# Attention values as one whole-array matmul a head plus 64x64 quarters, in one operation with the next tile's scores

## The chip, the cores and the metric

The kernel runs on one core of a Trainium2 chip. A core has a matrix engine (TensorE, PE in the profile; its weight loads are PEld), VectorE (DVE), ScalarE (ACT), GpSimd (POOL) and SyncE (SP), each with its own instruction stream, and 16 DMA engines that all queues share. The metric is the device time of one execution in microseconds (us), as the median of the runs. The profile is one further execution, taken by the hardware profiler; its span goes from the first to the last instruction.

## What is computed

Attention with a causal window of 128 keys and four sink keys (the first four of the sequence, which every query sees), over 4 batches, 8 heads, 768 positions, head size 64. Its output, with the heads side by side as 512 columns, goes through a layer norm, a two-layer MLP with 2048 hidden units and relu, and a residual.

```python
scores = scale * np.matmul(q, k.transpose(0, 1, 3, 2))
keep = is_sink | in_window                 # pos_k < 4, or 0 <= pos_q - pos_k < 128
a = softmax(np.where(keep, scores, -1e9))
attn_out = np.matmul(a, v)
...
xn = (x - mu) / np.sqrt(var + 1e-06) * g_ln
ch = np.maximum(xn @ w_ch1, 0.0) @ w_ch2
return x + ch
```

## The kernel before

A *tile* is 128 positions of one batch: 24 tiles (NT), six a batch (RB), numbered t; r is the tile's place in its batch. Two tiles are a *chunk* c, 12 in all (NC), three a batch (RC); R is the chunk's place in its batch, so R=0 opens one.

**Attention of a chunk** (chunks 2 to 11, `attend`; the four tiles of chunks 0 and 1 have `attend_tile`). Scores are computed transposed, with keys on the partitions and queries on the columns. For two of the four head pairs at a time (`half`), `bands` issues matmuls of 64 keys by 64 head dimensions (line 663): the two heads of a pair use the two row halves of the array, the two halves of the keys its two column halves, so that four run in the quarters of the array. Only blocks that touch the window are computed. With R=0, line 750 does it with 128 keys on 64 rows instead. The first half also computes the sinks' scores (line 754). The exponentials go to the tiles `pe` (line 764), a mask clears what lies outside the window (line 768), and `value` multiplies by V: for each head two whole-array matmuls of 65 columns (line 798), one over the own 128 keys and one over the 128 before, the 65th column of V being ones, which gives the row sum; and before them one 260-column matmul per four heads for the sinks (line 793, `vs` holding the sink values). In the first tile of a batch there is only one block of keys.

**After the values.** VectorE takes reciprocals (line 811), scales (813), takes the statistics (817, 819) and centres (821); POOL computes the inverse deviation (826, 827). The centred x is transposed, by TensorE in chunks 0 to 2 (834) and by a DMA on SP's queue from chunk 3 (836, by way of line 542), to `xnt`. q and k are transposed by TensorE up to chunk 3 (639) and by DMAs on SP's queue from chunk 4 (626).

**MLP of a chunk** (`mlp`): eight groups of eight matmuls for the first layer (line 867; 860 in chunk 0), each followed by a relu on ACT or DVE (877, 879); then for each tile four groups of four matmuls of 512 columns for the second layer (896), which DVE combines with the residual (904) and SP's queue stores (908).

**Loads.** q, k, v and the weights are loaded on POOL's queue, which casts to bf16 (lines 521, 524, 548, 600, 625, 634). The gain vector g is loaded transposed as 512 single elements (505).

**What sets the order.** Nothing is scheduled by hand: `Plan` holds every operation with its engine, an estimated duration, a priority and the buffers that it uses, and `Plan.run` walks through time, picks for each engine the ready operation of best priority within a short window, and hands out buffer slots. The operations are then emitted in order of their planned start, and each engine runs its own in that order, waiting on semaphores where data or a buffer isn't ready. `nb` is an earliest planned start. From priority `strict` on, TensorE's operations keep the order of their priorities. Priorities are in steps of 16 a chunk: `at(c, step)` is 16c - 8 plus an entry of `PAR`, and the MLP of a chunk starts at 16c + 8.5.

**PSUM.** Eight banks: two pairs of banks (`pair`, for scores and, from chunk 2, the values) and four single ones (`one`, for the MLP's layers, transposes and the sinks' scores).

Of the kernel before, what the change touches and what calls it, by code (L numbers as in the profile page):

```python
# [7 lines left out]
FP32 = mybir.dt.float32  # L8
# [5 lines left out]
class Buf:  # L14


    def __init__(self, name, ring=None):
        self.name, self.ring = name, ring
        self.writers, self.users = [], []
        self.slot = None  # L20
        self.left = 0

# [42 lines left out]
class Plan:  # L65
# [7 lines left out]
    SHARED = 36.0  # L73
# [8 lines left out]
    def op(self, name, engs, prio, emit, reads=(), writes=(), rw=(), dma=None, after=(), mode="n", hold=(), nb=0.0):  # L82
# [10 lines left out]
        o.bufs = list(dict.fromkeys(list(reads) + list(writes) + list(rw) + list(hold)))  # L93
# [19 lines left out]
    def run(self):  # L113
# [8 lines left out]
        while ready:  # L122
# [5 lines left out]
            for o in ready:  # L128
# [4 lines left out]
                for b in need:  # L133
# [9 lines left out]
                    avail = max(avail, s.free_at)  # L143
# [68 lines left out]
def fix(occ, extra=0.09):  # L212
# [3 lines left out]
SW = (0.9, 0.7, 0.9)  # L216
SW_W = (2.65, 0.7, 0.9)
# [4 lines left out]
HW_T = (0.10, 0.8, 0.8)  # L222
# [6 lines left out]
PAR = dict(strict=40.0, win=0.4, tr=-8.0, sc=-5.0, sc1=-2.0, av=2.0, trx=9.0, by_dma=4, x_by_dma=3,  # L229
           w1p=(1.6, 2.6, 2.7, 2.8), pm=3, w2p=(4.5, 4.51, 4.52, 4.53), apart=2, vs0=(2.0, 13.0), by_tile=1, vp=(0.0, 0.1, 2.0, 2.1, 4.55, 4.56), ld1=0.05)  # L230
# [135 lines left out]
def kernel(  # L366
# [63 lines left out]
    mask, mask0 = const("mask", [128, 2, 4, 128], BF16), const("mask0", [128, 2, 3, 128], BF16)  # L430
# [3 lines left out]
    vs = [const(f"vs{b}", [128, H, 65], BF16) for b in range(B)]  # L434
    gt = const("gt", [128, NDM], FP32)
# [9 lines left out]
    names = ("ident_f", "ident", "upper", "neg", "mask", "mask0", "sel", "vc", "vcd", "gt", "junk", "tab", "mhalf", "ones_f")  # L445
# [37 lines left out]
    def masks0(e):  # L483
        up = upper.unsqueeze(1).to_broadcast([128, 2, 128])
        V.tensor_copy(mask0[:, :, 0, :], up)
        V.tensor_scalar(mask0[:, :, 1, :], up, -1.0, 1.0, op0=ALU.mult, op1=ALU.add)
        V.tensor_copy(mask0[:, :, 2, :], up)
        V.memset(mask0[0:NS, :, 0:2, :], 1.0)

    def negs(e):  # L490
# [4 lines left out]
    constant("masks0", "DVE", 0.9, 6.1, masks0, ["upper"], writes=[Bc["mask0"]], nb=27.5)  # L495
# [4 lines left out]
        op=ALU.add, axis=mybir.AxisListType.X), ["ident"], writes=[Bc["sel"]])  # L500
    constant("mhalf", "DVE", 0.06, -52, lambda e: V.memset(mhalf, -0.5), writes=[Bc["mhalf"]])
# [3 lines left out]
    P.op("gt", {"SP": (0.4, 0.4)}, 3.0, lambda e: nc.sync.dma_start(gt, moe_g_ln.rearrange("(j p) -> p j", p=128)),  # L505
         writes=[Bc["gt"]], dma=HW_T)
# [5 lines left out]
    for b in range(B):  # L512
        P.op(f"vs{b}", {"DVE": dve(520)} if b else {"POOL": (0.9, 1.0)}, PAR["vs0"][0] if b == 0 else 48.0 * b - 20, lambda e, b=b: (V if b else G).tensor_tensor(
            vs[b], vc[:, b, :].unsqueeze(1).to_broadcast([128, H, 65]),
            sel.unsqueeze(2).to_broadcast([128, H, 65]), op=ALU.mult),
            reads=[Bc["vcd"], Bc["vc"], Bc["sel"]], writes=[Bvs[b]], nb=PAR["vs0"][1] if b == 0 else 40.0 * b)

    w1prio = PAR["w1p"]
# [25 lines left out]
    def load_v(t, prio):  # L544
# [5 lines left out]
            writes=[bv], dma=SW, after=list(ones_of.values()))  # L550
# [6 lines left out]
    def chunk(c):  # L557
# [57 lines left out]
        else:  # L615
            for nm, src, bT in (("k", k, kT_b), ("q", q, qT_b)):
# [3 lines left out]
                for i in range(2):  # L620
                    if c >= PAR["by_dma"]:
# [3 lines left out]
                             lambda e, nat=nat, ap=ap: G.dma_start(nat.t, ap), writes=[nat], dma=SW)  # L625
# [27 lines left out]
        for i in range(2):  # L653
            load_v(2 * c + i, ld + 0.3 + 0.1 * i if c >= RC else PAR["vp"][2 * c + i])
# [351 lines left out]
```

## Time and profile before

| | us |
|---|---|
| median of 3 runs | 220.07 (219.91 to 220.21) |
| profiled execution | 220.3 |
| its span | 218.7 |
| TensorE matmuls busy | 211.0 |
| VectorE busy | 117.9 |
| ScalarE busy | 108.2 |
| GpSimd busy | 90.2 |

The busy share of a stretch and the clock that TensorE was granted, in 40 slices of the span, in tenths:

```profile
PE   6889999999999999999999999999999999999993
DVE  5489845595797725725715815725716715732011
ACT  3768465145447447445546447445546447441610
POOL 7998673798091813463550722570110110120000
PEclk9999999999999999999999999999999999999998
DMA  5999999999999999799897999997523421121103
```

The granted clock is near full throughout (mean 0.997). The DMA engines are busy nine tenths or more of most slices up to some 155 us. The busiest groups of instructions:

```profile
L896 PE MATMUL one<-w,h 128*128 128x512 bf16 (+1 forms) x400 | 89.0, 371 | 0.0
L867 PE MATMUL one<-xnt,w 128*128 128x256 bf16 x704 | 82.4, 273 | 0.0
L798 PE MATMUL pair<-vn,pe 128*128 128x65 bf16 x296 | 12.2, 193 | 0.0
L663 PE MATMUL pair<-qT,kT 64*64 64x64 bf16 (+2 forms) x400 | 8.9, 219 | 0.1
L548 POOL DMA_DIRECT2D vn<-in_v_dram x24 | 21.9, 921 | 3.3 <-DMA w<-in_moe_w_ch_dram 3.1
```

A group's line gives the source line, the engine, what is written from what, and how often; then the busy time in us, the mean duration of one in ns, and the engine's idle time before them. Matmuls are pipelined: one of 512 columns lasts 0.37 us from start to end, while the next starts 0.216 us after it.

### The profile page before, as it was taken

The numbers are of one execution on the slowest core, as the hardware profiler recorded it, in microseconds if no ns is written. First come the engines' busy times: TensorE is split into PE (matmuls) and PEld (weight loads), VectorE is DVE, ScalarE is ACT, GpSimd is POOL, SyncE is SP. The second block draws the span as 40 slices with busy tenths as digits, with TensorE's granted clock in tenths as the row PEclk, the third lists the DMA queues.
The fourth block names the chain that finished last, engine by engine and source line by source line (L and its number), as shares of the span: only waits on it lengthen the run. The fifth ranks groups of instructions, "written<-read, shape, count | busy, mean of one in ns | idle before, by whom it ended". The sixth has DMA issues, their size and how long they took to land.

```text
span 218.7 us, 5474 instructions
## 1 busy us (share of the span) xinstructions
PE 211.0 (97%) x2233; PEld 144.6 (66%) x2233; DVE 117.9 (54%) x269; ACT 108.2 (49%) x162; POOL 90.2 (41%) x131
## 2 busy tenths in 40 slices
PE   6889999999999999999999999999999999999993
PEld 2557875764965964964965964964965965965852
DVE  5489845595797725725715815725716715732011
ACT  3768465145447447445546447445546447441610
POOL 7998673798091813463550722570110110120000
PEclk9999999999999999999999999999999999999998
DMA  5999999999999999799897999997523421121103
GB/s 155 163 183 207 176 206 197 156 211 154 179 159 163 139 120 129 100 160 145 139 135 116 133 115 129 135 140 106 129 40 98 107 41 48 51 48 51 48 12 101
DMA packets 108576, 27.47 MB, mean 126 GB/s; under 512 B 99200, under 2 KB 105600, under 8 KB 108544
## 3 DMA queue, kind: packets, MB, share of 16 engines
q0 software_dynamic: 74944, 13.11, 83.7%
q1 hardware_dynamic: 32544, 13.41, 30.2%
q10 hardware_dynamic: 1056, 0.52, 0.9%
q8 instruction: 19, 0.31, 0.6%
q14 instruction: 13, 0.11, 0.2%
HBM read 27.30 MB, written 6.29 MB: 154 GB/s over the span
## 4 chain that ended last, share of the span: by engine, by line
PE 90%; DVE 6%; issue 1%; ACT 1%; DVEq 0%
PE one L896 39%; PE one L867 35%; PE pair L798 4%; PE pair L663 3%; PE pair L962 2%; PE pair L793 1%; DVE st L817 1%; PE pair L750 1%; DVE x L813 1%; DVE xc L821 1%; DVE xnt L845 1%; PE one L639 1%; PE one L860 1%; PE one L834 1%; PE one L754 1%
## 5 line engine op out<-in xcount | busy, mean ns | idle before, releaser
L896 PE MATMUL one<-w,h 128*128 128x512 bf16 (+1 forms) x400 | 89.0, 371 | 0.0
L877 ACT ACTIVATE h<-one 128x512 bf16<-128x512 f32 x95 | 56.6, 598 | 59.1 <-PE one L867 50.7
L867 PE MATMUL one<-xnt,w 128*128 128x256 bf16 x704 | 82.4, 273 | 0.0
L867 PEld LDWEIGHTS <-w 128*128 128x128 bf16 x704 | 67.4, 98 | 10.2
L896 PEld LDWEIGHTS <-h 128*128 128x128 bf16 x400 | 37.3, 98 | 38.2 <-issue 0.9
L768 DVE TENSOR_TENSOR pe<-pe,mask 128x1024 bf16<-128x1024 bf16 (+1 forms) x40 | 26.0, 649 | 54.7 <-ACT pe L764 53.8
L764 ACT ACTIVATE pe<-pair 128x1024 bf16<-128x1024 f32 (+1 forms) x40 | 36.2, 957 | 33.4 <-PE pair L663 21.6
L625 POOL DMA_DIRECT2D nat<-in_k_dram x16 | 14.2, 890 | 36.8 <-DMA kT<-nat 28.1
L904 DVE SCALAR_TENSOR_TENSOR ot<-one,st,x 128x512 f32<-128x512 f32 (+1 forms) x25 | 18.1, 725 | 15.2 <-PE one L896 15.1
L826 POOL TENSOR_SCALAR st<-st 128x1 f32<-128x1 f32 x24 | 7.1, 297 | 43.4 <-DVE st L819 42.2
L548 POOL DMA_DIRECT2D vn<-in_v_dram x24 | 21.9, 921 | 3.3 <-DMA w<-in_moe_w_ch_dram 3.1
L625 POOL DMA_DIRECT2D nat<-in_q_dram x16 | 14.6, 913 | 12.9 <-DMA qT<-nat 12.0
L817 DVE BATCH_NORM_STATS2 st<-x 128x6 f32<-128x512 bf16 x24 | 16.7, 695 | 0.8
L798 PEld LDWEIGHTS <-pe 128*128 128x128 bf16 x352 | 14.0, 97 | 2.1 <-ACT pe L709 0.6
L827 POOL TENSOR_TENSOR st<-st,mhalf 128x1 f32<-128x1 f32 x24 | 14.3, 596 | 2.0
L813 DVE TENSOR_TENSOR x<-pair,rec 128x512 bf16<-128x512 f32 x20 | 13.8, 691 | 0.7
L798 PE MATMUL pair<-vn,pe 128*128 128x65 bf16 x296 | 12.2, 193 | 0.0
L663 PEld LDWEIGHTS <-kT 64*64 64x64 bf16 x400 | 6.2, 107 | 6.3 <-issue 6.1
L821 DVE TENSOR_SCALAR xc<-x,st 128x512 bf16<-128x512 bf16 x24 | 9.3, 389 | 0.9
L811 DVE RECIPROCAL rec<-pair 128x8 f32<-128x8 f32 x20 | 4.0, 202 | 9.7 <-PE pair L798 9.7
L709 ACT ACTIVATE pe<-pair 128x1024 bf16<-128x1024 f32 (+1 forms) x8 | 7.3, 919 | 3.5 <-PE pair L663 2.1
L663 PE MATMUL pair<-qT,kT 64*64 64x64 bf16 (+2 forms) x400 | 8.9, 219 | 0.1
(87 smaller groups left out, 127.4 us busy)
## 6 DMA issues: line engine op xcount, KB each, us to landing
out_dram<-ot SPq DMA_DIRECT2D x23, 256.0 KB
w<-in_moe_w_ch_dram POOLq DMA_DIRECT2D x8, 512.0 KB, 12.9
vn<-in_v_dram POOLq DMA_DIRECT2D x24, 128.0 KB, 6.3
nat<-in_k_dram POOLq DMA_DIRECT2D x22, 128.0 KB, 6.1
nat<-in_q_dram POOLq DMA_DIRECT2D x22, 128.0 KB, 6.2
natf<-in_k_dram SPq DMA_DIRECT2D x2, 256.0 KB
natf<-in_q_dram ACTq DMA_DIRECT2D x2, 256.0 KB
xnt<-xc SPq DMA_TRANSPOSE x18
```

The source lines that it names most:

```text
L548: P.op(f"vld{t}", {"POOL": (0.87, 0.9)}, prio, lambda e: G.dma_start(bv.t[:, :, 0:64], v[b, :, 128 * r:128 * (r + 1), :].rearrange("h p d ...
L625: lambda e, nat=nat, ap=ap: G.dma_start(nat.t, ap), writes=[nat], dma=SW)
L663: nc.tensor.matmul(pp.t[64 * kh:64 * kh + 64, h2, col + off:col + off + n], lhsT=kt.t[rs, hp, k0 + 64 * kh:k0 + 64 * kh + 64], rhs=qT.t[rs ...
L764: P.op(f"ex{c}{hp}", {"ACT": act(2 * n)}, d + 0.1 + 0.05 * j, lambda e, pp=pp, pb=pb: nc.scalar.activation(pb.t[:, :, 0:n], pp.t[:, :, 0:n ...
L768: V.tensor_tensor(pb.t[:, :, 0:n], pb.t[:, :, 0:n], mm, op=ALU.min if R else ALU.mult),
L798: nc.tensor.matmul(bank(h // 4)[:, 65 * (h % 4):65 * (h % 4) + 65], lhsT=part(h, n), rhs=vn_b[tv].t[:, h, :], start=(not R and h % 4 == 0 ...
L813: P.op(f"x{t}{run[0]}", {"DVE": dve(512 * share)}, dd + 0.11, lambda e, pv=pv, rc=rc, run=run: V.tensor_tensor(x.t[:, 256 * run[0]:256 * r ...
L817: P.op(f"bn{t}", {"DVE": fix(0.60)}, d + 0.12, lambda e: V.bn_stats(st.t[:, 8:14], x.t), reads=[x], writes=[st, mv])
L867: nc.tensor.matmul(ph.t[:, 256 * s:256 * s + 256], lhsT=w1[ht // 4][:, j, 128 * (ht % 4):128 * (ht % 4 + 1)], rhs=xnt.t[:, j, :], start=j ...
L877: nc.scalar.activation(hb.t, ph.t, AF.Relu)
L896: nc.tensor.matmul(pc.t[:, 0:wd], lhsT=(h1[2 * s + i].t[:, 128 * ii:128 * ii + 128] if by_tile else h1[ht // 2].t[:, 256 * (ht % 2) + 128 ...
L904: V.scalar_tensor_tensor(ot.t[:, sl], in0=pc.t[:, 0:wd], scalar=st.t[:, 16:17], in1=x.t[:, sl], op0=ALU.mult, op1=ALU.add),
```

## The change

For chunks 3 to 11 (batches 2 to 4) `attend` is replaced by `block`, one operation a tile. `block(t)` first finishes the values of tile t-1 and then computes the scores of tile t; `block(NT)` closes with values alone. `attend` stays for chunk 2.

The keys of a tile are regrouped. With 64-key halves, the queries' own tile has the halves 0 and 1 and the tile before it -2 and -1. Halves -1 and 0 are seen, in part, by all 128 queries: they are the *middle 128 keys*, stacked on the 128 partitions, and one whole-array matmul a head covers them. Half -2 matters only to the first 64 queries and half 1 only to the last 64: each is a 64x64 quarter. For heads 0 to 3 (u=0) and 4 to 7 (u=1) the two halves are stacked in opposite order, so that the quarters of both use all four quarters of the array. The sinks' values become four quarters of 260 columns, for which the sink values are also kept with their halves swapped (`vs_s`, made by six DMAs on SP's queue). V is loaded in the shifted stacking by `load_m`, in three or four DMAs a tile.

The exponentials and masks of a tile cover 768 columns in two instructions each; the masks are a product with `band` or, in a batch's first two tiles, `edge`, built by `bands3`. The first tile of a batch also runs the middle matmul and half of the quarters over keys of the batch before, with zeros in the masked places. The sinks' scores of a chunk are computed with its first tile.

PSUM now has three pairs; the third is two of the four single banks, which the planner lends (`lent`) to operations that come before the next waiting `block`. Second-layer sums from chunk 2 on use only the two others (`acc`). `lag` lets a score bank be handed out although it comes free a little after the operation's start. `strict` is raised, so that the order of priorities no longer binds TensorE; loads of V from tile 10 and of q and k from chunk 5 are planned no earlier than 58 us; the transposes of chunk 4 no longer wait for the scores of chunk 3. The gain vector is loaded as four rows and transposed by TensorE.

```diff
-        o.bufs = list(dict.fromkeys(list(reads) + list(writes) + list(rw) + list(hold)))
+        o.bufs = sorted(dict.fromkeys(list(reads) + list(writes) + list(rw) + list(hold)), key=lambda b: b.ring != "pair")
...
-                    avail = max(avail, s.free_at)
+                    avail = max(avail, s.free_at - b.lag)
...
+PAR = dict(strict=400.0, late=58.0, win=0.4, tr=-8.0, sc=-5.0, sc1=-2.0, av=2.0, blk=-8.0, step=6.0, trx=9.0, by_dma=4, x_by_dma=3,
...
-    pairs = [psum.tile([128, 2, 512], FP32, name=f"pair{i}") for i in range(2)]
-    ones = [psum.tile([128, 512], FP32, name=f"one{i}") for i in range(4)]
-    P.ring("pair", [Slot(pairs[i], f"pair{i}", banks[2 * i:2 * i + 2]) for i in range(2)])
-    P.ring("one", [Slot(ones[i], f"one{i}", [banks[4 + i]]) for i in range(4)])
+    pairs = [psum.tile([128, 2, 512], FP32, name=f"pair{i}") for i in range(3)]
+    ones = [pairs[2][:, i, :] for i in range(2)] + [psum.tile([128, 512], FP32, name=f"one{i}") for i in range(2, 4)]
+    P.ring("two", [Slot(pairs[i], f"two{i}", banks[2 * i:2 * i + 2]) for i in range(2)])
+    P.ring("pair", [Slot(pairs[i], f"pair{i}", banks[2 * i:2 * i + 2]) for i in range(3)])
+    P.ring("one", [Slot(ones[i], f"one{i}", [banks[4 + i]], rank=0, lent=i < 2) for i in range(4)])
+    P.ring("acc", [Slot(ones[i], f"acc{i}", [banks[4 + i]]) for i in range(2, 4)])
...
+    def bands3(e):
+        for u in range(2):
+            m = edge[1][u]
+            for g in range(2):
+                rows = slice(64 * g, 64 * g + 64)
+                up, at = upper[rows, 64 * g:64 * g + 64], [0, 128] if g == u else [128, 64]
+                V.tensor_copy(m[rows, at[0]:at[0] + 64], up)
+                V.tensor_scalar(m[rows, at[1]:at[1] + 64], up, -1.0, 1.0, op0=ALU.mult, op1=ALU.add)
+                V.memset(m[rows, 64:128] if g == u else m[rows, 0:64], 1.0)
+            own = 64 * u
+            V.tensor_copy(band[u], m.unsqueeze(1).to_broadcast([128, 4, 192]))
+            V.tensor_copy(edge[0][u], m)
+            V.memset(m[own:own + NS, 128:192], 0.0)
+            V.memset(edge[0][u][64 - own:128 - own, 0:128], 0.0)
+            V.memset(edge[0][u][own:own + 64, 128:192], 0.0)
+            V.memset(edge[0][u][own:own + NS, 0:128], 1.0)
...
+    constant("bands3", "DVE", 3.0, 6.1, bands3, ["upper"], writes=[Bc["band"]], nb=28.0)
...
+    P.op("gt", {"SP": (0.4, 0.4)}, 3.0, lambda e: nc.sync.dma_start(g_rows, moe_g_ln.rearrange("(j p) -> j p", p=128)),
+         writes=[gr_b], dma=HW_T)
+    P.op("gtt", pe(0.1), PAR["gtt"], lambda e: nc.tensor.transpose(gt_p.t[:, 0:NDM], g_rows, ident_f[0:NDM, 0:NDM]),
+         reads=[gr_b, Bc["ident_f"]], writes=[gt_p])
+    P.op("gtc", {"DVE": fix(0.07)}, PAR["gtt"] + 0.1, lambda e: V.tensor_copy(gt, gt_p.t[:, 0:NDM]), reads=[gt_p], writes=[Bc["gt"]])
...
+    Bvt = [None] + [Buf(f"vt{b}") for b in range(1, B)]
+    for b in range(1, B):
+        for g in range(2):
+            P.op(f"vt{b}{g}", {"SP": (0.35, 0.4)}, 48.0 * b - 19.5, lambda e, b=b, g=g: nc.sync.dma_start(
+                vs_s[b][64 * g:64 * g + 64], vs[b][64 * (1 - g):64 * (1 - g) + 64]), reads=[Bvs[b]], writes=[Bvt[b]], dma=HW_V)
...
-            writes=[bv], dma=SW, after=list(ones_of.values()))
...
+    def load_m(t, prio):
...
+        if r:
+            parts = [(0, 128, hi, at(b, s0 - 64, 128, hi)), (0, 64, lo, at(b, s0, 64, lo)), (64, 64, lo, at(b, s0 - 64, 64, lo))]
+        else:
+            pb = (t - 1) // RB
+            parts = [(0, 64, hi, at(pb, S - 64, 64, hi)), (64, 64, lo, at(pb, S - 64, 64, lo))]
+            if t < NT:
+                parts += [(64, 64, hi, at(b, 0, 64, hi)), (0, 64, lo, at(b, 0, 64, lo))]
+        for i, (p0, n, hs, src) in enumerate(parts):
+            P.op(f"vld{t}_{i}", {"POOL": (0.8, 0.85)}, prio + 0.001 * i, lambda e, p0=p0, n=n, hs=hs, src=src: G.dma_start(
+                m.t[p0:p0 + n, hs, 0:64], src), writes=[m], dma=SW_H if n == 128 else SW_Q, after=list(ones_of.values()),
...
-                             after=[scores[c - 1]])
+                             after=[scores[c - 1]] if c > PAR["by_dma"] else [])
...
+    def block(t):
...
+        d = at(c, "blk") + PAR["step"] * i
...
+            po = Buf(f"po{t - 1}", "pair")
+            reads += last["pes"] + ([last["ps"], Bvs[lb], Bvt[lb]] if last["ps"] else [])
+            reads += [vn_b[u] for u in ([t - 2, t - 1, t] if lr else [t - 1, t])]
+            writes.insert(0, po)
+            for j, pp in enumerate(pps if t < NT else ()):
+                pp.lag = (0.5 if last["ps"] else 0.4) + 0.15 * j
+            hold += last["made"]
...
+        def at_p(j, h):
+            return last["pes"][j].t.rearrange("p a b -> p (a b)"), 192 * (2 * (h % 2) + h // 2 % 2)
+
+        def go(e):
+            for h in range(H) if last else ():
+                pe_, col = at_p(h // 4, h)
+                nc.tensor.matmul(po.t[:, h // 4, 65 * (h % 4):65 * (h % 4) + 65], lhsT=pe_[:, col:col + 128],
+                                 rhs=vn_b[t - 1].t[:, h, :], start=h % 4 == 0, stop=True, skip_group_check=True)
+            if last and last["ps"]:
+                for u in range(2):
+                    for qh in range(2):
+                        g = qh ^ u
+                        rs = slice(64 * g, 64 * g + 64)
+                        nc.tensor.matmul(po.t[64 * qh:64 * qh + 64, u, 0:260],
+                                         lhsT=last["ps"].t[rs, 128 * u + 64 * li:128 * u + 64 * li + 64],
+                                         rhs=(vs if g == u else vs_s)[lb][rs].rearrange("p h c -> p (h c)"),
+                                         start=False, stop=True, skip_group_check=True)
+            for h in [4 * u + i for i in range(4) for u in range(2)] if last else ():
+                for qh in (0, 1) if lr else (1,):
+                    g = qh ^ (h // 4)
+                    rs = slice(64 * g, 64 * g + 64)
+                    pe_, col = at_p(h // 4, h)
+                    nc.tensor.matmul(po.t[64 * qh:64 * qh + 64, h // 4, 65 * (h % 4):65 * (h % 4) + 65],
+                                     lhsT=pe_[rs, col + 128:col + 192], rhs=vn_b[t if qh else t - 2].t[rs, h, :],
+                                     start=False, stop=True, skip_group_check=True)
+            if t == NT:
+                return
+            for hp in range(HP):
+                u, col = hp // 2, 192 * (hp % 2)
+                for g, kt, k0, c0, q0, n in ((u, kT, own, 0, own, 128), (1 - u, kprev, old + 64, 0, own, 128),
+                                             *([(u, kprev, old, 128, own, 64)] if r else []), (1 - u, kT, own + 64, 128, own + 64, 64)):
+                    for h2 in range(2):
+                        rs = slice(64 * h2, 64 * h2 + 64)
+                        nc.tensor.matmul(pps[u].t[64 * g:64 * g + 64, h2, col + c0:col + c0 + n],
+                                         lhsT=kt.t[rs, hp, k0:k0 + 64], rhs=qT.t[rs, hp, q0:q0 + n],
+                                         start=col + c0 == 0, stop=True, skip_group_check=True)
+            if sinks:
+                for hp in range(HP):
+                    for qh in range(2):
+                        u = hp // 2
+                        p0 = 64 * (qh ^ u) + 32 * (hp % 2)
+                        nc.tensor.matmul(pp_s.t[p0:p0 + 32, 128 * u + 64 * (not r):128 * u + 128], lhsT=kts_b[b].t[:, hp, :],
+                                         rhs=qT.t[:, hp, :].rearrange("p (i u c) -> p u i c", i=2, u=2)[:, qh, 0 if r else 1:2],
+                                         start=True, stop=True, skip_group_check=True)
+        cost = (0.0 if t == NT else 0.32 if r else 0.29) + (0.0 if not last else 0.35 + (0.12 if lr else 0.11) + (0.115 if last["ps"] else 0.0))
+        end = t < NT and sinks
+        P.op(f"sc{t}", pe(cost + ((0.2 if r else 0.15) if end else 0)), d, go, reads=reads, writes=writes, hold=hold, mode=("n" if last else "q", "c" if end else "q"))
...
+                    nc.scalar.activation(pes[j].t.rearrange("p a b -> p (a b)")[:, 0:768].rearrange("p (a b) -> p a b", a=2),
+                                         pps[j].t[:, :, 0:384], AF.Exp, scale=scale)
...
+                    V.tensor_mul(at_s, at_s, band[j] if r > 1 else edge[r][j].unsqueeze(1).to_broadcast([128, 4, 192]))
...
-                pc = Buf(f"pc{t}{f}", "one")
+                pc = Buf(f"pc{t}{f}", "one" if c < 2 else "acc")
...
+        elif c < RC:
+            attend(c)
         else:
-            attend(c)
+            block(2 * c)
+            block(2 * c + 1)
+    block(NT)
```

More of the change, by code (lines that the diff above doesn't have):

```diff
@@ L500 @@
         op=ALU.add, axis=mybir.AxisListType.X), ["ident"], writes=[Bc["sel"]])
+    constant("sel4", "DVE", 0.1, 6.0, lambda e: V.tensor_tensor(sel4, sel[:, 0:4], sel[:, 4:8], op=ALU.add),
+             ["sel"], writes=[Bc["sel4"]], nb=27.0)
     constant("mhalf", "DVE", 0.06, -52, lambda e: V.memset(mhalf, -0.5), writes=[Bc["mhalf"]])
@@ L677, in attend_tile @@
             if t or j == 0:
-                pp, pb = Buf(f"s{t}{j}", "pair"), Buf(f"p{t}{j}", "pe")
+                pp, pb = Buf(f"s{t}{j}", "two"), Buf(f"p{t}{j}", "pe")
                 pes.append(pb)
@@ L755, in sc @@
                                          rhs=qT.t[:, hp, :], start=True, stop=True, skip_group_check=True)
-            sinks = R and half == 0
-            scores[c] = P.op(f"sc{c}{half}", pe(0.33 if R else 2 * n / 2400) if not sinks else pe(0.54), d, sc,
-                 reads=[kT, qT] + ([kprev] if R else [])
+            sinks = half == 0
+            scores[c] = P.op(f"sc{c}{half}", pe(0.54 if sinks else 0.33), d, sc,
+                 reads=[kT, qT, kprev]
                  + ([kts_b[b]] if sinks else []), writes=pps + ([pp_s] if sinks else []),
-                 hold=pbs + ([ps] if sinks else []), mode=("q", "c") if sinks else "q" if R else "r")
+                 hold=pbs + ([ps] if sinks else []), mode=("q", "c") if sinks else "q")
             for j, pp in enumerate(pps):
@@ L785, in value @@
         recs.append(rcb)
-        whole = Buf(f"po{t}", "pair") if c >= PAR["apart"] else None
+        whole = Buf(f"po{t}", "two") if c >= PAR["apart"] else None
         for run in [(0, 1)] if whole else [(0,), (1,)]:
```

142 lines of the change are left out of this document (98 added, 44 removed).

## The prediction

> **What bounds the kernel now.** I read the page's busy shares first, then TensorE's waits, then the chain of waits piece by piece, then single instructions around one attention chunk.
>
> ```profile
> PE 211.0 (97%) x2233; PEld 144.6 (66%) x2233; DVE 117.9 (54%) x269; ACT 108.2 (49%) x162; POOL 90.2 (41%) x131
> ```
>
> TensorE is busy 97% of the span, and its waits are short and early:
>
> ```profile
> PE pair L962 <- DVE one_e L458: 1.8, 1, 1.8
> PE one L834 <- DVE xc L821: 0.9, 2, 0.6
> PE pair L684 <- ACT pe L709: 0.4, 1, 0.4
> PE pair L703 <- ACT qT L554: 0.2, 1, 0.2
> ```
>
> The last of them ends at 25.58 us (tile 3's x being centred). From there to 214.97 us the chain is TensorE alone, piece touching piece; then 3.7 us follow for the last output tile. So between 26 and 215 us a microsecond taken from TensorE's instruction stream is a microsecond off the time, as long as nothing new makes it wait. This is the chain in one chunk of batch 2 (start, length, instructions):
>
> ```profile
> 79.06 2.59 PE one L896 x12
> 81.64 0.46 PE pair L663 x24
> 82.11 0.22 PE one L754 x4
> 82.33 2.70 PE one L896 x12
> 85.03 0.46 PE pair L663 x22
> 85.49 1.83 PE one L896 x8
> 87.32 1.75 PE one L867 x16
> 89.07 0.22 PE pair L793 x2
> 89.29 0.48 PE pair L798 x16
> ```
>
> Twelve L896 cost 2.59 us alone and 2.70 us right after scores, so leaving the 64x64 layout costs 0.11. Entering costs about as much: the single-instruction records put 0.094 us between the end of the L896 stream and the first L663. A score half is then 0.343 us from its first to its last start, plus 0.028 for the last 64 columns. From end of MLP stream to MLP stream again, averaged over the six chunks with a previous chunk in their batch (R>0): **0.791** for the half with sinks, **0.568** for the other, **0.709** for one tile's values (0.22 sinks, 16 x 0.030). Sum 0.791 + 0.568 + 2 x 0.709 = 2.777 a chunk. The three chunks that open batches 2 to 4 (R=0):
>
> ```profile
> 98.31 0.44 PE pair L750 x8
> 98.75 2.70 PE one L896 x12
> 101.45 0.44 PE pair L750 x8
> ...
> 105.46 0.26 PE pair L798 x8
> 105.72 0.87 PE one L867 x8
> 106.59 0.48 PE pair L798 x16
> ```
>
> They cost 2 x 0.544 + 0.259 + 0.485 = 1.832. All nine chunks: 6 x 2.777 + 3 x 1.832 = **22.2 us** of TensorE, which the change replaces.
>
> **The change, part by part.** One operation per tile now runs the previous tile's values and this tile's scores. Its terms for an inner tile:
> - whole-array values: 8 instead of 16 at 0.0295 = 0.236;
> - entry to 64x64: 0.094;
> - sinks as four 64x64 quarters of 260 columns: side by side 260/2.4 = 0.108, taken 0.113 (L896 steps 0.2155 for 512 columns, L867 0.1092 for 256: 2.4 columns a ns plus 3 ns);
> - 16 diagonal quarters of 65 columns, four deep in each quarter of the array: 4 x 0.0295 = 0.118;
> - 32 score matmuls, 768 columns in each quarter as in the old half: 0.345 (0.371 less 0.026, since the old half's first step of 64 columns took 0.053 with no weights ahead of it, and here other quarters run before);
> - exit 0.104.
>
> Sum 1.01 us. A tile that opens a chunk adds the sinks' scores: one more switch 0.092 and 0.115, so 1.22; with R=0 they have half the columns, 0.152 in all. A tile after a batch's first has no sinks in its values: 0.90. Nineteen operations: tile 6 (scores only) 0.67; tiles 12 and 18, 1.14 each; three of 0.90; six of 1.22; six of 1.01; the closing one (values only) 0.67. Together 0.67 + 2.28 + 2.69 + 7.30 + 6.06 + 0.67 = **19.7 us**. Gain 22.2 - 19.7 = **2.5 us**. It comes from values (0.709 to about 0.47); the columns of scores and the number of switches stay.
>
> No run of before has 65-column quarters in a row, so that price is bounded. Below: 65 columns in 0.027, gain 0.2 more. Above: the 0.053 just named, which is a step whose weights were not loaded early; 18 x 4 x 0.024 = 1.7 less. I take the lower row's side, because at 81.745 and 81.773 two starts in one quarter stand 0.028 apart after 64 columns, in mid-stream as here. The Trainium skill, "TensorE: Matmul & The Clock Gate", section "LDWEIGHTS", gives a load as columns/1.2 ns, 53 ns for 64; by that the gain would be 0.8 us. The mid-stream step of 28 ns speaks against it.
>
> **Banks.** Eight PSUM banks remain, but the third pair is two of the four single banks. A tile's operation takes all three pairs, and every second one starts where a first MLP layer has just ended:
>
> ```profile
> 127.95 1.24 PE L896 MATMUL one<-w,h 128*128 128x512 bf16 x5
> 128.21 0.60 ACT L877 ACTIVATE h<-one 128x512 bf16<-128x512 f32 x1 [0.28 <-PE one L867]
> ```
>
> The last bank is read until 128.81, 0.86 us after the next work starts. The new operation writes its second score tile 0.236 + 0.094 + 0.113 + 0.118 + 0.17 = 0.73 after its start. If that tile has this bank, TensorE waits some 0.2 us with the semaphore; otherwise none. Nine such places: 0 to 2 us; I take **0.4**.
>
> **Loads.** V comes shifted by 64 rows, in 59 DMAs on POOL's queue instead of 18 (45 for 15 inner tiles, 14 for the batch edges), 41 more of 0.913 us: POOL goes from 90 to 128 us of 219. The same bytes move. Loads of tiles from 10 and chunks from 5 stand later in that queue, behind the r.m.s. work of earlier tiles; what they delay are the transposes of q and k on SP's queue, which the old order issues some 10 us ahead of use (135 for scores at 147). Six DMAs that copy the sink values stand on SP's queue and wait for DVE's product (0.69), with transposes behind them. I cost both at nothing while that lead holds; without it TensorE waits for the lateness itself, 0 to 3 us.
>
> **Start.** The gain vector's load turns from 512 packets of 4 bytes (0.5 us of all engines near 6.2 us) into four rows, a small PE transpose and a DVE copy. Up to 25.6 us DVE sets the pace: minus 0.3 to plus 0.3, taken 0. The new masks are 24 DVE instructions instead of four (1.26 us from 26.62 to 27.88): 3 to 5 us after 28, where DVE was idle for 2.7 of 4.1 us and evictions can go to ACT. Hidden while TensorE has the rest of the first two chunks' MLP to run (some 20 us of L867 and L896); without that cover up to 1. Exponentials shrink from 1.02 to 0.81 us and masks from 0.69 to 0.56, off the path.
>
> **Sum.** The profiled execution took 220.3 with a span of 218.7; the median is 220.07, 0.2 lower. Span 218.7 - 2.5 + 0.4 = 216.6; on the median 220.07 - 2.1 = **218.0 us**.
>
> **Rivals.**
> 1. *Transposed x comes late* (slower). Values of a chunk's second tile move from 13 us ahead of its MLP (122.87 against 136.21) to 9.15 us: that operation 1.22, six L896 groups 5.19, the next operation 1.01, two groups 1.73. In that time run 0.84 to the values' end, 2.3 on DVE (122.21 to 124.47) and the DMA transpose, whose last packet left 1.9 us after issue in quiet stretches and 6.0 at 75.49 and 5.7 at 124.50, when POOL's loads ran beside it. 0.8 + 2.3 + 6.0 = 9.1: just inside. With a mean of 0.6 us over at nine chunks, 218.0 + 5.4 = 223.4; it turns the gain from 0.25 us a chunk on. For it: more load DMAs; against it: most landed within 4.4. Price taken 221 to 223.
> 2. *Quarters of one bank don't run together* (slower). Scores of before send the two row halves to two banks; the diagonal quarters send both halves into one bank, at different partitions. If those take turns, sinks cost 0.11 more and quarters 0.12 more in 15 tiles: 3.4, so 218.0 + 3.4 = 221.4. The Trainium skill, "TensorEngine Tiling (Array Packing)", "Gotcha 1: PSUM Pressure", says that different row tiles cannot access one PSUM bank at the same time. Against: nothing in this trace tests it; the four column strips of L754 do share a bank and start 3 ns apart.
> 3. *Quarters at 0.053*: 218.0 + 1.7 = 219.7.
> 4. *The bank wait in full*: 0.2 and more at all 18 tiles, 219.5 to 220.5; against it, only half of those places follow a first layer.
>
> **Numbers.** Forecast 0.60, its own range 217.2 to 218.9 (start and banks). Rival 1: 0.12; 2: 0.08; 3: 0.10; 4: 0.10. About 0.2% (0.44 us, so 219.63 to 220.51) can be told from no change. Faster: 0.60, most of 3 and half of 4, some of 1 at a small wait: 0.70. Same 0.07, slower 0.23. The range 217.0 to 221.2 reaches down to start and banks at their best (218.0 - 0.4 - 0.3 - 0.2 with quarters at 0.027 is 217.1) and up through rivals 3 and 4 to part of 1 and 2.
>
> **What would show it.** TensorE's waits after 26 us stay under 1 us; the chain shows eight whole-array value matmuls, some 0.24 us, then one run of quarters about 0.6 to 0.8 us; the next MLP group after it is 0.11 longer. Wrong would be: TensorE waiting for ACT's relu or exponentials (banks), for a DMA of xnt at the first L867 of a chunk (rival 1), or value quarters whose starts stand 50 ns apart (3) or in twos (2).

## The result and the profile after

| | before | after |
|---|---|---|
| median, us | 220.07 (5 runs, 219.91 to 220.21) | 221.7 (5 runs, 221.06 to 222.28) |
| ratio, 95% interval | | 1.007 (1.0045 to 1.0094) |
| profiled execution, its span, us | 220.3, 218.7 | 221.8, 220.2 |

The change makes the kernel 0.7% slower; I had forecast 218.0. Here and below, ratios leave out executions more than 1.5% above a kernel's fastest, while medians and ranges keep them. The page's busy line of after (engine, busy us, share of the span, instructions):

```profile
PE 211.1 (96%) x2678; PEld 147.4 (67%) x2678; DVE 115.4 (52%) x289; ACT 101.3 (46%) x167; POOL 116.8 (53%) x172
```

TensorE is as busy as before (211.0), in a span that is 1.5 us longer: the 1.5 us are time in which it does nothing. TensorE's waits of after (waiting line and what it waits for: total us, times, longest):

```profile
PE pair L1127 <- DVE one_e L468: 1.8, 1, 1.8
PE pair L839 <- ACT h L1038: 1.0, 1, 1.0
PE pair L689 <- ACT h L1038: 0.7, 1, 0.7
PE pair L739 <- ACT pe L764: 0.6, 1, 0.6
PE one L884 <- DVE xc L871: 0.4, 1, 0.4
PE pair L758 <- ACT qT L604: 0.2, 1, 0.2
PE pair L633 <- ACT kT L604: 0.2, 1, 0.2
PE pair L972 <- DVE kts L700: 0.2, 1, 0.2
```

New are the second, third, seventh and eighth lines, 2.1 us, all on `pair` and all before 52 us. The eighth is a true wait (the sinks' scores read `kts`). The others can't be: values (839) and transposes of k (689) neither read nor replace what a relu (1038) reads: in the program the values write the first half of the pair's tile and the relu reads the second, and the transposes write the second half and the relu reads the first. Two stretches of the timeline show how they arise (start, length, engine, line, [idle before it, and what ended that]). First the opening transposes of k and q (633) and their evictions (604):

```profile
5.57 1.06 PE L633 MATMUL pair<-ident,natc 128*128 128x128 bf16 x4
6.34 0.73 PE L739 MATMUL pair<-neg,ident 128*128 128x512 bf16 x2
7.30 0.60 PE L633 MATMUL pair<-ident,natc 128*128 128x128 bf16 x4 [0.23 <-ACT kT L604]
```

The transposes of q at 7.30 write one bank. They wait until ACT has read k's transposes out of another one. In before's program the same matmuls wait for nothing there:

```
before: L583 Matmult one1_64<-ident,natc1_70 128x128
after:  L633 Matmult pair2_63<-ident,natc1_69 128x128   [waits Activation]
```

The two single banks that the change took for the third pair are now views of one tile (`pairs[2][:, i, :]`), and the order between instructions is kept per tile: a write to one half waits for the readers of the other. Then the transposes of chunk 2 beside the relus of chunk 0, ACT first, then PE:

```profile
29.83 0.60 ACT L1038 ACTIVATE h<-pair 128x512 bf16<-128x512 f32 x1 [0.63 <-PE pair L689]
30.89 1.01 ACT L604 COPY kT<-pair 128x1024 bf16<-128x1024 bf16 x1 [0.47 <-PE pair L689]
```

```profile
29.40 0.39 PE L689 MATMUL pair<-ident,nat 128*128 128x128 bf16 x4
30.47 0.38 PE L689 MATMUL pair<-ident,nat 128*128 128x128 bf16 x4 [0.68 <-ACT h L1038]
30.92 0.82 PE L1028 MATMUL one<-xnt,w 128*128 128x256 bf16 x6
```

The relu waits for transposes that write the other half, and the next transposes wait for that relu: a chain from half to half. The three false waits (1.0, 0.7 and 0.2) are 1.9 us, all before chunk 1's first layer.

Past 52 us TensorE waits for nothing, and the chain of waits is TensorE piece by piece as before (start, length, what):

```profile
113.70 0.26 PE pair L937 x8
113.96 0.23 PE pair L944 x4
114.20 0.13 PE pair L953 x16
114.33 0.35 PE pair L964 x32
114.67 0.23 PE one L972 x8
114.90 5.29 PE one L1057 x24
120.19 0.26 PE pair L937 x8
120.44 0.23 PE pair L944 x4
120.68 0.13 PE pair L953 x16
120.81 0.35 PE pair L964 x32
121.16 1.83 PE one L1057 x8
```

That is a chunk-opening tile (113.70 to 114.90) and an inner one (120.19 to 121.16): 937 whole values, 944 the sinks' quarters with the entry to 64x64, 953 the diagonal quarters, 964 scores, 972 the sinks' scores.

**Where the time went.** I follow the MLP, whose matmuls are the same in all kernels. The first first-layer matmul of chunk 1 starts at 28.27 us before and at 30.92 after: 2.65 lost. From there to the last second-layer matmul take 186.36 and 185.57 us: 0.79 won. From the start of that matmul to the end of the span before takes 4.05 us and after 3.71. 2.65 - 0.79 - 0.34 = 1.5, the difference of the spans. It is not the change that won the 0.34: in before's profile VectorE's last operation starts 0.73 us after that matmul, in after's 0.31, and in e3's, a run of before with one small edit, 0.38.

### The profile page after: what moved, and what is told of

It reads as the page before. It is cut to its first block, busy times and chain, and to the rows that moved or that the text cites. A ratio compares the mean times of both kernels' runs of the same rounds, so it can differ in the third digit from the quotient of the medians.

```text
span 220.2 us, 6412 instructions
## 1 busy us (share of the span) xinstructions
PE 211.1 (96%) x2678; PEld 147.4 (67%) x2678; DVE 115.4 (52%) x289; ACT 101.3 (46%) x167; POOL 116.8 (53%) x172
## 4 chain that ended last, share of the span: by engine, by line
PE 91%; DVE 4%; ACT 2%; issue 0%; DVEq 0%
PE one L1057 36%; PE one L1028 17%; PE pair L1028 17%; PE pair L964 3%; PE pair L937 2%; PE pair L1127 2%; PE pair L1021 2%; PE pair L944 2%; PE pair L1057 2%; PE pair L953 1%; ACT kT L604 1%; PE one L1021 1%; DVE x L859 1%; PE one L972 1%; PE pair L739 1%; PE pair L689 1%
## 5 line engine op out<-in xcount | busy, mean ns | idle before, releaser
L982 ACT ACTIVATE pe<-pair 128x768 bf16<-128x768 f32 x36 | 27.2, 808 | 43.1 <-issue 28.1
L598 POOL DMA_DIRECT2D vn<-in_v_dram x59 | 39.0, 681 | 12.3 <-PE pair L964 7.0
L1028 PE MATMUL one<-xnt,w 128*128 128x256 bf16 x352 | 43.7, 273 | 0.0
L1038 ACT ACTIVATE h<-pair 128x512 bf16<-128x512 f32 x47 | 25.8, 595 | 37.3 <-PE pair L1028 33.9
L1028 PE MATMUL pair<-xnt,w 128*128 128x256 bf16 x352 | 42.2, 273 | 0.0
L1038 ACT ACTIVATE h<-one 128x512 bf16<-128x512 f32 x48 | 28.7, 601 | 16.8 <-PE one L1028 14.7
L987 DVE TENSOR_TENSOR pe<-pe,band 128x768 bf16<-128x768 bf16 x24 | 12.2, 550 | 0.0
L964 PE MATMUL pair<-qT,kT 64*64 64x128 bf16 (+1 forms) x552 | 9.5, 205 | 0.0
L764 ACT ACTIVATE pe<-pair 128x1024 bf16<-128x1024 f32 (+1 forms) x8 | 7.2, 918 | 3.7 <-PE pair L718 2.0
L937 PEld LDWEIGHTS <-pe 128*128 128x128 bf16 x144 | 7.0, 98 | 2.3
```

What stands on the lines that cost most here:

```text
L598: P.op(f"vld{t}_{i}", {"POOL": (0.8, 0.85)}, prio + 0.001 * i, lambda e, p0=p0, n=n, hs=hs, src=src: G.dma_start(m.t[p0:p0 + n, hs, 0:64], ...
L964: nc.tensor.matmul(pps[u].t[64 * g:64 * g + 64, h2, col + c0:col + c0 + n], lhsT=kt.t[rs, hp, k0:k0 + 64], rhs=qT.t[rs, hp, q0:q0 + n], st ...
L982: nc.scalar.activation(pes[j].t.rearrange("p a b -> p (a b)")[:, 0:768].rearrange("p (a b) -> p a b", a=2), pps[j].t[:, :, 0:384], AF.Exp, ...
L987: V.tensor_mul(at_s, at_s, band[j] if r > 1 else edge[r][j].unsqueeze(1).to_broadcast([128, 4, 192]))
L1028: nc.tensor.matmul(ph.t[:, 256 * s:256 * s + 256], lhsT=w1[ht // 4][:, j, 128 * (ht % 4):128 * (ht % 4 + 1)], rhs=xnt.t[:, j, :], start=j ...
L1038: nc.scalar.activation(hb.t, ph.t, AF.Relu)
```

## The experiments

For all twelve profiles, in us: when TensorE reached full clock (the trace's clock records; until then the 512-column warm-up matmuls stand 0.427 apart, later ones of that size 0.2155), when chunk 1's first layer starts, and how long it is from there to the start of the last second-layer matmul.

| kernel | time (median) | full clock at | chunk 1's first layer | from there on |
|---|---|---|---|---|
| before | 220.07 | 5.74 | 28.27 | 186.36 |
| after | 221.7 | 6.52 | 30.92 | 185.57 |
| e0 after again | 221.81 | 5.05 | 30.37 | 185.57 |
| e1 before, shared tile | 228.93 | 6.02 | 31.24 | 192.07 |
| e2 separate banks | 220.29 | 7.07 | 28.77 | 185.43 |
| e3 before, gain as rows | 220.23 | 6.66 | 28.47 | 186.36 |
| e4 separate banks again | 220.45 | 7.08 | 28.76 | 185.32 |
| e5 three single banks | 221.09 | 5.12 | 29.97 | 185.50 |
| e6 no diagonal quarters | 217.41 | 5.35 | 27.93 | 186.96 |
| e7 separate, 1 us earlier | 218.98 | 4.49 | 27.91 | 185.21 |
| e8 separate, 2 us earlier | 221.16 | 6.81 | 28.54 | 187.44 |
| e9 shared, 1 us earlier | 221.57 | 5.00 | 30.22 | 185.57 |

Before was run again beside e0 to e3 (220.22), e4 to e7 (220.13) and e8 and e9 (220.22).

**e0: after, unchanged.** The rival cause of the slow start was the clock, which in the profile of after came up 0.8 us later than in that of before.

> The changed kernel once more, with a profile of its own. Theory A (the third score pair shares one tile with two of the four single banks, and work on one half waits for readers of the other half): TensorE waits again for ACT's eviction of kT at some 7 us, for a relu before the values at some 20 us and before the transposes at some 30 us, and stands 2.3 to 3.0 us behind the kernel before at 32 us. Rival B (the start was slow because the clock came up 0.8 us later in that profile): with a clock that comes up at 5.7 us the lag at 17 us shrinks from 1.0 to under 0.5 us and the time falls towards 221.0.

221.81 (221.4 to 222.25), ratio 1.0082 (1.0064 to 1.01). Now the clock was up at 5.05, before before's 5.74, and chunk 1's first layer is still 2.10 late. The first MLP matmul moved as the rival said, from 17.09 to 16.54 (before 16.08), but the time did not follow. The clock accounts for some 0.5 us of the start (30.92 against 30.37) and not for the loss.

**e1: before, with nothing but the sharing added.**

```diff
-    pairs = [psum.tile([128, 2, 512], FP32, name=f"pair{i}") for i in range(2)]
-    ones = [psum.tile([128, 512], FP32, name=f"one{i}") for i in range(4)]
+    pairs = [psum.tile([128, 2, 512], FP32, name=f"pair{i}") for i in range(3)]
+    ones = [pairs[2][:, i, :] for i in range(2)] + [psum.tile([128, 512], FP32, name=f"one{i}") for i in range(2, 4)]
```

> The kernel before, with one edit: two of its four single banks are views of one two-bank tile, as in the changed kernel; attention is the old one. Theory A: the start loses what it lost in the changed kernel, 2.3 to 3.0 us, so 222.4 to 223.1 us, with the same waits of TensorE for ACT in the first 32 us. If only the new attention or the later clock is to blame: 220.1 within 0.4.

228.93 (228.74 to 229.0), ratio 1.0402 (1.0388 to 1.0415): much more than expected. Some of its waits of TensorE:

```profile
PE pair L896 <- ACT h L877: 1.4, 2, 0.7
PE pair L896 <- DVE ot L904: 0.9, 2, 0.5
```

The start lost 2.97, as in after, but 5.7 more went later. In before's order the second layer (896) uses these halves too; the change keeps it on the two other banks (the `acc` ring), which I had not counted as protection. Sharing one tile is by itself enough for the loss.

**e2: after, with separate banks.** Four tiles of one bank again; values go to two of them instead of a third pair, so their division takes four VectorE instructions a tile instead of two.

```diff
-    ones = [pairs[2][:, i, :] for i in range(2)] + [psum.tile([128, 512], FP32, name=f"one{i}") for i in range(2, 4)]
+    ones = [psum.tile([128, 512], FP32, name=f"one{i}") for i in range(4)]
...
-            po = Buf(f"po{t - 1}", "pair")
+            po = [Buf(f"po{t - 1}{u}", "one") for u in range(2)]
```

> The changed kernel with four separate single banks and two pairs; a tile's values go to two single banks, so that reciprocal and scaling become two VectorE instructions each. Theory A: the start is as before and the values' gain of some 1.1 us is left: 221.7 - 2.6 = 219.1, 218.7 to 219.5. If the sharing is not to blame: 221.2 to 222.2. If banks run short in the steady part (values and sinks' scores now take three of four single ones): over 220, with TensorE waiting for ACT's relu at every second tile.

The waits of TensorE that its profile lists:

```profile
PE pair L1129 <- DVE one_e L468: 1.8, 1, 1.8
PE one L884 <- DVE xc L871: 0.8, 2, 0.6
PE pair L739 <- ACT pe L764: 0.6, 1, 0.6
PE pair L758 <- ACT qT L604: 0.2, 1, 0.2
```

The false waits are gone. Chunk 1's first layer is 0.50 late, with the latest clock but one of the table, and 0.93 is won from there on. The median is nevertheless 220.29 (12 runs, 218.62 to 223.77), ratio 0.9999 (0.9975 to 1.0023), above what I expected, with a spread that neither before nor after has. It is over 220, as if banks ran short, but the waits for relus that were to show that are not there.

The profiled execution took 220.75, and its span is 0.57 longer than before's, though 0.50 - 0.93 would make it 0.43 shorter. The other 1.0 us lies at the end. VectorE's last operation in e2 (span 219.3) and in before (span 218.7):

```profile
214.51 0.48 DVE L1067 SCALAR_TENSOR_TENSOR ot<-one,st,x 128x256 f32<-128x256 f32 x1 [0.66 <-PE one L1059]
215.36 0.48 DVE L904 SCALAR_TENSOR_TENSOR ot<-one,st,x 128x256 f32<-128x256 f32 x1 [1.08 <-PE one L896]
```

From the end of that operation to the end of the span e2 takes 4.26 us, before 2.84, after 2.92. A DMA lands in sixteen parts by the trace's records; of the last output store fifteen had landed at 217.01, the sixteenth came at 218.16, and SyncE, which waits for it, ends the kernel 1.1 us after that. In before the last two parts are 0.14 apart.

**e3: before, with the gain vector as four rows and a PE transpose.**

> The kernel before, with the gain vector loaded as four rows and transposed by TensorE as in the changed kernel. If this edit is part of the slow start: 220.4 to 221.0. If it is off the path, as predicted: 219.8 to 220.4.

220.23, ratio 0.9998 (0.9986 to 1.001). That part of the change is off the path.

**e4: e2 once more.**

> The kernel with four separate single banks once more, to settle its median (220.29, from 218.62 to 223.77 so far). Shared-tile theory (the start loses through waits for the other half, the new blocks gain 1.1 in the steady part): lag to before at 8 us of first- and second-layer work 0.2 to 0.8, gain after 27 us 1.0 to 1.15, so 219.0 to 219.9. Rival, that something else than the shared tile gives the gain back: 220.1 to 220.6 and a stall in the steady part that the first profile did not show, or a tail after the last VectorE operation of 4 us and more again (before 2.9).

220.45 (218.86 to 223.70), ratio 0.9991 (0.9969 to 1.0012): the rival's number, and one of the two signs that it named. Start and steady gain repeat e2's to 0.1 us, and TensorE waits for no more than there (its list also has nine gaps of some 0.16 us in the second layer; there the trace lacks matmul records, 377 of 400). But the tail after VectorE's last operation is 4.34 us: the last store's sixteenth part landed at 218.12, 0.96 after the fifteenth. So the separate banks give back most of what the start lost, and in these two profiles the end takes back 1.0 and 1.1 us.

**e5: after, with only one half of the third pair lent.**

```diff
-    P.ring("one", [Slot(ones[i], f"one{i}", [banks[4 + i]], rank=0, lent=i < 2) for i in range(4)])
+    P.ring("one", [Slot(ones[i], f"one{i}", [banks[4 + i]], rank=0, lent=i < 2) for i in (0, 2, 3)])
```

> The changed kernel, but only one half of the third pair is lent as a single bank (three single banks instead of four), so that no two buffers ever lie in one tile at a time. Shared-tile theory: the waits for the other half (1.0 + 0.7 + 0.2 us in the profile of the changed kernel) are gone, lag to before at 8 us of first- and second-layer work 0.3 to 1.0 instead of 2.65, time 219.3 to 220.4. Rival, that the start suffers from too few single banks whatever tile they lie in: the lag stays at 2 or grows, 221.5 to 223.

221.09, ratio 1.0045 (1.0029 to 1.0061); chunk 1's first layer 1.70 late, between the two expectations. The waits for the other half are gone, but with three single banks the start is held up in its own right (TensorE waits 2.1 us for the centred x, 0.9 in before, and its first MLP matmul comes at 19.32, in after at 17.09). It doesn't decide between the two.

**e6: e2 without the 264 diagonal quarters.**

```diff
-            for h in [4 * u + i for i in range(4) for u in range(2)] if last else ():
+            for h in [4 * u + i for i in range(4) for u in range(2)] if last and NEVER > 0 else ():
```

> The kernel with four separate single banks, with the 264 diagonal 64x64 quarters of the values left out (the outer 64 keys on each side of a query then do not count in the values). If the blocks are paid in full on TensorE, 15 tiles at 0.129 and 3 at 0.065 us go, 2.1 us: the gain after 27 us grows from 1.1 to 3.2. If the end is set by something else (the transposes of x, the loads), less than 0.5 us. If the quarters only fill gaps between the whole-array matmuls and the scores, 1.0 or less.

217.41 against e4's 220.45, 3.0 less; of the lowest times, 217.06 against 218.86, 1.8. In the profile the chunks are shorter by the quarters' price: 15.79 from one first layer to the next (138.26 to 154.05) where e4 has 16.04, two tiles at 0.13. So they are paid in full on TensorE. (From chunk 1 on the profile has 186.96; without the stall of 3.7 described next that is 183.26, 2.06 less than e4, where 2.1 was expected.) But the profiled execution was the slowest of the five, 220.49, and shows what made it slow. One line of its waits, and two of its windows (window, its length, busy us of PE, PEld, DVE, ACT and POOL, granted clock, DMA, GB/s):

```profile
PE one L1030 <- DMA xnt<-xc: 2.0, 1, 2.0
```

```profile
70.00:75.00 5.00, 3.01 (x19) 1.93 (x18) 2.73 (x6) 0.94 (x2) 4.84 (x8) 0.86 2.46 166
75.00:80.00 5.00, 5.00 (x38) 4.11 (x37) 0.00 (x0) 2.51 (x5) 4.56 (x7) 0.80 1.80 215
```

The first layer of chunk 3 waited from 70.77 to 72.76 for the DMA transpose of x that had been issued at 66.91. Then the clock went down: the records have 0.5 from 73.62 to 77.03, 3.41 us, which cost 1.7 more. So one late transpose cost 3.7 us here. By the landing records fifteen of its parts came by 71.22, the last at 72.72, 0.05 us before the matmul that waited for it. In e2 the same transpose landed 0.05 us before its first use, which is the same: TensorE waited there too, for 0.11 us (0.323 from the last second-layer matmul to the first of chunk 3, elsewhere 0.216), too little for the list of waits. In e5 the transpose of chunk 4 was late in the same way (0.461 instead of 0.216). In e4 it had 0.56 to spare (the last part 0.78 after the others), in after 2.88, in before 2.49. With separate banks the start is faster, and TensorE comes to chunk 3 just as x does.

**e7: e2, with each block due 1 us earlier.**

```diff
-PAR = dict(..., blk=-8.0, ...)
+PAR = dict(..., blk=-9.0, ...)
```

> The kernel with four separate single banks, with every block due 1 us earlier in the plan. If the wide spread of its times comes from transposes of x that land late in some executions (margins to first use 1.4 to 3.9 us in its profile, 3.8 to 7.6 before), the margins grow by about 1 us, the spread falls under 1.5 us and the median by 0.2 to 0.8. If not: median within 0.2 of the kernel with separate banks, spread as there.

218.98 (12 runs, 218.64 to 220.28), ratio 0.9946 (0.9929 to 0.9964): faster than both kernels. Its lowest time is e2's (218.64 and 218.62); what is gone are the long executions. The spread is 1.64, just over the 1.5 of the expectation, and the median fell by 1.3 to 1.5, more than it said. Of the profile's lead over e4, 0.85 lies in the start, with the clock up 2.6 us sooner, and only 0.1 in the steady part; its end has the late part too (1.09 after the fifteenth, 4.20 from VectorE's last operation), and at 219.62 it is one of the longer of the twelve. At chunk 3, x now lands 2.55 us ahead of its use, by the thirteen landings that the trace has of it: issued 5.3 us ahead (e2 4.7, e4 5.1), and landed 2.8 after issue (e2 4.6, e4 4.5). Most of the margin is the quicker landing, and one profile does not show whether the earlier blocks brought it. The other chunks' margins did not grow (1.63 to 2.92; in e4 1.65 to 3.42), against the expectation, but only chunk 3 had next to none. (The margins in the expectations, 1.4 to 3.9 and 3.8 to 7.6, were to the last packet; the landings, on which TensorE waits, come later.)

**e8: the same, 2 us earlier** (`blk=-10.0`).

> Four separate single banks and every block due 2 us earlier than in the changed kernel (1 us gave 218.98, from 218.64 to 220.28). If margins of the transposes of x were what widened the times, a further microsecond gives at most 0.3 more (218.6 to 219.0, spread 1 or less), since the steady gain is the same. Rival: the blocks now come before their own loads and transposes of q and k (0.5 to 4 us from the last packet to the first use in the profiles): waits of TensorE for those, 219.5 to 222.

221.16, ratio 1.0046 (1.0023 to 1.0069): the rival's number by another wait. Not q and k are late, but banks:

```profile
PE one L1059 <- DVE x L1007: 0.9, 3, 0.3
```

```profile
127.70 1.92 PE L1030 MATMUL one<-xnt,w 128*128 128x256 bf16 x16
129.94 3.61 PE L1059 MATMUL one<-w,h 128*128 128x512 bf16 x15 [0.31 <-DVE x L1007]
```

The second layer starts in a bank whose values VectorE is still dividing. Three chunks are 0.47 to 0.48 longer than e7's by that; the other five are 0.09 to 0.24 longer, for which I have no line.

**e9: after, shared tile kept, blocks 1 us earlier** (the edit of e7 alone).

> The changed kernel with the shared third pair kept, blocks due 1 us earlier. Shared-tile theory: the start is as in the changed kernel (first- and second-layer work at 8 us 2 to 2.7 behind before), and its times were narrow already, so 220.9 to 221.8. Rival, that the due time and not the shared tile was what the separate banks with earlier blocks gained: 219 to 220.

221.57 (221.02 to 222.11), ratio 1.006 (1.0045 to 1.0076). It has the waits of after (1.0, 0.7, 0.2 and 0.2), and chunk 1's first layer is 1.95 late. Earlier blocks alone win nothing.

## Why the prediction was wrong

**Start: the step that failed.** "Up to 25.6 us DVE sets the pace: minus 0.3 to plus 0.3, taken 0." It was plus 2.65. I had looked there at the gain vector, which costs nothing (e3), and at the masks (bands3, some 4.5 us of VectorE from 28.4), during which TensorE shows no wait for them. I had not asked what the new PSUM layout does to the first chunks, though in these the lent banks hold transposes, relus and values side by side. Shown three ways: the sharing alone, put into before, costs 2.97 there (e1); taken out of after, 2.15 of 2.65 come back (e2, e4), and all of it in e6 and e7, which run the same instructions up to there and have 27.93 and 27.91 with the clock up at 5.35 and 4.49; with it, the loss stays under an early clock (e0) and under another due time (e9).

**Banks: right object, wrong wait.** I priced the third pair as a bank read too long at nine places in the steady part, 0.4. There TensorE waits for nothing after 52 us. The price was order between the halves of a tile, and my list of steps had no term for it.

**The blocks: right mechanism, term too small.** 19.7 predicted, about 21.1 measured, so 1.1 instead of 2.5. In the steady part all came as the chain was said to show it. From MLP stream to MLP stream the inner tile takes 1.077 (I said 1.01), the chunk-opening one 1.302 (1.22), tiles 12 and 18 1.19 (1.14), the ones without sinks 0.96 (0.90), the closing one 0.73 (0.67). The parts, read from the starts of one tile:

| term | predicted | measured |
|---|---|---|
| eight whole values | 0.236 | 0.26 |
| entry to 64x64 | 0.094 | 0.093 |
| sinks' quarters | 0.113 | 0.135 |
| 16 diagonal quarters | 0.118 | 0.129 |
| 32 score matmuls | 0.345 | 0.358 |
| exit | 0.104 | 0.103 |

Nothing is far off: the two switches are as predicted, the other four terms 0.01 to 0.025 more, the whole-array values most (0.0325 each, where 16 in a row took 0.0295). The sinks' quarters have 0.010 between the first and the fourth start, which my price left out. Eighteen tiles multiply that. The removed part was right: 22.2.

With the start at 0 and the blocks as measured, after would have been 1.1 faster than before by its span; with the blocks as predicted and the start as measured, about equal. Neither error alone gives the result: -2.1 + 2.65 + 1.4 - 0.4 = +1.55, against +1.5 measured. Two smaller terms nearly cancel: the 0.34 at the end, and some 0.3 more after chunk 1's start, 0.2 of it the wait for `kts`.

**The rivals.** *Quarters of one bank take turns* and *quarters at 0.053* are refuted by the timeline of after:

```profile
130.16 0.29 PE L944 MATMUL pair<-vs,ps 64*64 64x260 bf16 x1
130.16 0.30 PE L944 MATMUL pair<-vs_s,ps 64*64 64x260 bf16 x1
130.17 0.29 PE L944 MATMUL pair<-vs,ps 64*64 64x260 bf16 x1
130.17 0.30 PE L944 MATMUL pair<-vs_s,ps 64*64 64x260 bf16 x1
130.30 0.30 PE L953 MATMUL pair<-vn,pe 64*64 64x65 bf16 x16
130.43 0.52 PE L964 MATMUL pair<-qT,kT 64*64 64x128 bf16 x32
```

The four sinks' quarters start within 0.01 us, two row halves in each bank, and the sixteen diagonal ones take 0.13, four deep: 0.032 a step. *Transposed x late*: not in the profile of after, where x lands 1.5 to 3.75 us ahead (before 2.5 to 7.1); but margins did shrink, as the rival said, and one execution of e6 shows it in full, with the price of a changed clock on top that I didn't have; e2 and e5 show 0.11 and 0.25 us of it. *Bank wait in full*: not in after; e8 waits for banks at three places, in the second layer. I was right on loads too: POOL went to 116.8 us (I said 128; a V load takes 0.681, not 0.913), and TensorE waits for none of them.

**Open.** That a late transpose at chunk 3 makes an execution long is shown by one execution of e6. The three longest of e2 and e4 (223.29, 223.70 and 223.77) carry its mark: a mean clock of 0.990 or 0.991, e6's being 0.992, where their other 21 have 0.995 or more. That it is the same transpose there is argued, from the missing margin and from e7, which has the margin and not the long times. The two profiles, of executions at 220.75 and 220.72, show the late last part of the output store instead, 1.15 and 0.96 us; why it comes so late in e2, e4 and e7, and at most 0.30 after the fifteenth in the other nine profiles, is open, and so is how often it does. What part the clock's start has in the shorter differences was not separated.

## What to carry to other kernels

Before two buffers are made views of one tile, list who writes and reads them everywhere, the first microseconds above all: order is kept per tile, so each half inherits the waits of the other, and an order planned by banks doesn't see it. Where that is the price, separate tiles and two more small VectorE instructions were cheaper (2.15 us at the start). A block that saves columns by many short matmuls should be priced with steps from runs of that length, and a forecast gain of 11% of the attention (2.5 of 22.2 us) shrinks to 5% when four of six terms are 0.01 to 0.025 us more than their nearest row. When times spread, read a profile to its last event: the chain that ends at the last operation of an engine leaves out the landing of the last store (in e2 it ends at 214.99 us of 219.25).

## What the runs showed of the hardware

TensorE reached full clock between 4.49 and 7.08 us in twelve profiles; that moved chunk 1's first layer by up to 0.85 us between kernels with the same start (e4 and e7), twice what 0.2% of the time is. The spans of full clock in the records are whole multiples of one length: 211.626 us is 62 x 3.4133, 215.040 is 63, and e6's 68.267 is 20, followed by one at half rate, 3.413. The Trainium skill, "TensorE: Matmul & The Clock Gate", section "What's actually happening", gives that window, 3413 ns, free-running, and lets the clock fall after at least one idle window; here 2.0 us without matmuls were enough, in a window (70.21 to 73.62) in which TensorE had worked 1.4 us.

Of a DMA's sixteen landing records the last two mostly stand within 0.05 us of each other, but not always: of the transposes of x, the last part came 1.50 us after the fifteenth in e6 (chunk 3), 1.86 in e8 (chunk 6) and 1.20 in e1 (chunk 3), and of the last store 0.96 to 1.15 in e2, e4 and e7. In e6 TensorE started 0.05 us after the last one.
